# The values' round trip through DRAM: one copy in token order against eight copies by place and chunk, with the next values' load moved behind the reads

## The chip, the core and the metric

The kernel runs on one core of a Trainium2 chip. The metric is device time in microseconds; the kernel before takes 360.43 us (median of three runs, 359.46 to 362.16). One further execution was taken with the hardware profiler: 358.42 us, of which 356.7 us lie between its first and last instruction. All times inside the kernel are from that execution.

## What is computed

Chunked attention with a few memory keys, followed by a mixture of experts that gives every token its two best experts of eight. Cut to what matters:

```python
# attention: batch 4, heads 8, seq 768, head_dim 64, 8 memory keys
for c in range(24):                        # chunks of 32 queries
    l_start, r_end = max(0, 32*c - 16), min(768, 32*c + 32 + 8)
    k_full = concat(mem_k, k[l_start:r_end]); v_full = concat(mem_v, v[l_start:r_end])
    a = softmax(q[32*c:32*c+32] @ k_full.T / 8)
    out[32*c:32*c+32] = a @ v_full
# experts: 3072 tokens of 512, hidden size 1024
x = out.transpose(0, 2, 1, 3).reshape(3072, 512)
noisy = x @ w_gate + log1p(exp(x @ w_noise)) * noise
top2, weights = two largest of noisy, softmax over them
result = sum over the two experts e: weight * (relu(x @ w1[e]) @ w2[e])
```

Each chunk sees a window of 56 tokens: 16 to its left, its own 32, 8 to its right. With the 8 memory keys that makes 64 keys a chunk.

## The kernel before

The kernel has an attention stage and an expert stage. The attention stage runs over four batches of 768 tokens, each in three tiles of 256 tokens (twelve tiles, index `i`, in the loop at L562). For each tile TensorE makes the scores (`scores`, L402), VectorE takes the maximum and the difference (L423, L425), ScalarE the exponential (L430), TensorE turns the probabilities (`turn_p`, L433) and multiplies them by the values (`values`, L442, the product at L453), VectorE divides into the token rows (L460), and TensorE turns these and makes the gate's logits (`turn_x`, `gate`). The routing's small VectorE operations are strewn between the tiles. Then tokens are sorted by their pair of experts, gathered (L671), and sent through the two matmuls of the expert stage (L714, L726) and scattered to the output (L677).

Queries, keys and values of a batch are loaded by GpSimd's DMA queue with a conversion from float32 to bfloat16 (`load_nat`, L116; `load_v`, L119; `load_kq`, L122). A partition holds six neighbouring tokens of each head, so a piece in memory is 6 x 64 elements, 768 B once converted. Queries and keys are turned by TensorE (`turn`, L387, the transposes at L393) into `qT` and `kT`.

The values need no turning, but for the product at L453 the window of each chunk has to lie on the partitions: partition = place in the window, free axis = chunk and channel. The kernel makes this by a round trip through DRAM, in three steps:

- `spread_v` (L366, copies at L368): GpSimd brings the loaded values `vn` from head order into token rows of 512 channels, `vp`, in two copies, one for even and one for odd heads.
- `window_v`, first line (L374): one DMA on SP's queue writes `vp` to the DRAM tile `vd` (two of them, used in turn), as 16 rows of zeros, 768 token rows of 1 KB, 16 rows of zeros. A partition's six rows are one run of 6 KB. The zeros are written once at the start (L156).
- `window_v`, the rest: two DMAs put the memory values on 8 partitions (L378), and four DMAs read the windows back (L383, called spans below): for the even and the odd heads, the first 32 places and the last 24 places. One descriptor is 512 B, half a row; successive chunks of one place lie 32 rows (32 KB) apart. They fill `vb` (two of them, used in turn).

The order of transfers is set by the program order on the queues: `pin` keeps GpSimd's instructions as written, and SP's engine follows its written order too. GpSimd's order is: values, keys, queries of batch 0; spread 0; memory values and spans 0; values, queries, keys of batch 1; spread 1; **values of batch 2** (L535); then, at the first tile of batch b (L567 to L573): memory values and spans of b + 1; queries and keys of b + 2; spread of b + 2; **values of b + 3**. After the last spans come the loads of experts 0 to 2 (`load_expert`, L575, L578), later the gathers of tokens and the other experts, all on the same queue. The spans wait for SP's copy to have landed; SP's copy waits for the spread; the spread waits for the values.

`vn`, `vb` and the buffers of queries and keys lie in the part of the weights' tile `w_all` that later experts fill, which is why the profile shows loads, spans and products on `w_all`.

Of the kernel before, what the change touches and what calls it, by code (L numbers as in the profile page):

```python
# [12 lines left out]
BF16 = mybir.dt.bfloat16  # L13
# [9 lines left out]
def kernel(  # L23
# [14 lines left out]
    nc = tc.nc  # L38
    B, H, S, D = q.shape
# [30 lines left out]
    def pin(i):  # L70
        tc.keep_in_program_order(i)
# [36 lines left out]
    vn = scratch(H * SO * D).rearrange("p (h c) -> p h c", h=H)  # L108
    vb = [scratch(2 * NCH * HP * D).rearrange("p (a c w) -> p a c w", a=2, c=NCH) for _ in range(2)][::-1]
# [3 lines left out]

    vd = [tc.dram_tile([S + CH, Dm], BF16, name=f"vd{i}") for i in range(2)]

    def load_nat(t, x, b):  # L116
        pin(nc.gpsimd.dma_start(out=t, in_=x[b].rearrange("h (p s) d -> p h (s d)", s=SO)))

    def load_v(b):  # L119
        load_nat(vn, v, b)  # L120

    def load_kq(b):  # L122
        for x in ((1, 0) if b else (0, 1)):
            load_nat(nat[b % 2][x], (k, q)[x], b)
# [24 lines left out]
    nc.vector.tensor_copy(identf, identb[0:NG, 0:NG])  # L149
    vp = keep.tile([128, H * SO * D], BF16, name="vp")  # L150
    lg_all = keep.tile([128, NG, 2 * E], F32, name="lg_all")
    zeros = keep.tile([128, Dm], BF16, name="zeros")
    nc.vector.memset(zeros, 0.0)
    for i in range(2):
        for r0, n in ((0, LC), (LC + S, CH - LC)):
            nc.sync.dma_start(out=vd[i][r0:r0 + n, :], in_=zeros[0:n, :])  # L156


    mks = keep.tile([128, 2, D], F32, name="mks")
# [206 lines left out]
    def spread_v(b):  # L366
        for par in range(2):
            pin(nc.gpsimd.tensor_copy(  # L368
                out=vp.rearrange("p (s a c d) -> p a c s d", s=SO, a=2, c=HP)[:, par],
                in_=vn.rearrange("p (c a) (s d) -> p a c s d", a=2, s=SO)[:, par]))  # L370

    def window_v(b):
        t, o = vb[b % 2], vd[b % 2]
        nc.sync.dma_start(out=o[LC:LC + S, :].rearrange("(p s) c -> p (s c)", s=SO), in_=vp)  # L374
        for par in range(2):
            p0 = par * 64
            cols = slice(par * 256, (par + 1) * 256)
            pin(nc.gpsimd.dma_start(out=t[p0:p0 + NM, par], in_=mvn[b * NM:(b + 1) * NM, cols].unsqueeze(1).to_broadcast([NM, NCH, 256])))  # L378
        for par in range(2):
            p0 = par * 64  # L380
            cols = slice(par * 256, (par + 1) * 256)
            for r0, n in ((0, CH), (CH, WIN - CH)):
                pin(nc.gpsimd.dma_start(out=t[p0 + NM + r0:p0 + NM + r0 + n, par],  # L383
                                        in_=o[r0:r0 + S, cols].rearrange("(c k) w -> k c w", k=CH)[0:n]))

# [130 lines left out]
    with tc.manual_schedule(engines={ET.PE, ET.Activation, ET.DVE, ET.SP}):  # L516
# [17 lines left out]
        spread_v(1)  # L534
        load_v(2)  # L535
        pbs[0] = exps(scores(0))
# [25 lines left out]
        for i in range(NT):  # L562
# [423 lines left out]
```

## Time and profile before

| | |
|---|---|
| median of 3 runs | 360.43 us |
| profiled execution | 358.42 us |
| its span | 356.7 us |
| busy in the span: TensorE | 285.9 us (80%) |
| VectorE | 170.3 us (48%) |
| ScalarE | 136.9 us (38%) |
| GpSimd | 134.3 us (38%) |
| GpSimd's DMA queue (q0) | 34240 packets, 46.82 MB |
| SP's DMA queue (q1) | 13920 packets, 6.62 MB |
| mean granted clock of TensorE | 0.867 |

How to read it: the page gives busy time by engine, then the span in 40 slices of 8.9 us with a digit for the busy tenths of each. The attention stage fills the first 16 slices or so. A row of the timeline has start, duration, engine, line, operation, written and read tiles, and in brackets how long the engine had been idle and what ended that. A row of the DMA view for a window counts the packets that were moved in it; "software_dynamic" is GpSimd's queue, "hardware_dynamic" those of SP and ScalarE.

### The profile page before, as it was taken

What the parts mean: (1) busy time and instruction counts of PE and PEld (TensorE: products, weight loads), DVE (VectorE), ACT (ScalarE), POOL (GpSimd) and SP (SyncE); (2) the same over time, 40 slices, a digit from 0 to 9 for tenths busy, and PEclk for the clock granted to TensorE, in tenths of its full rate; (3) what the DMA queues carried; (4) which work ended last, traced back from release to release, by engine and by line L of the source; (5) the groups of instructions that cost most, each with busy time, mean ns of one, the idle gap of its engine ahead of it and who ended that gap; (6) DMA issues with size and microseconds to landing.
All of it is one profiled execution on the core that took longest, in us unless ns stands there. A gap on an engine that the chain in (4) does not pass through costs nothing.

```text
span 356.7 us, 7042 instructions
## 1 busy us (share of the span) xinstructions
PE 285.9 (80%) x2934; PEld 186.3 (52%) x2955; DVE 170.3 (48%) x349; ACT 136.9 (38%) x189; POOL 134.3 (38%) x181
## 2 busy tenths in 40 slices
PE   0356577777847732999999999999999999999991
PEld 0245455666736621865544465664455775565540
DVE  7656456699689885531133302954310334223221
ACT  8813645564645610144322343213243222243310
POOL 6460573354453036706530744332580122201122
PEclk9995655565687865699999999999999999999998
DMA  8999999999999999499999999961289971100012
GB/s 122 235 171 169 245 174 208 251 198 211 247 156 208 253 249 180 106 194 143 178 196 235 209 173 252 159 119 51 87 166 189 208 184 54 53 2 2 25 47 81
DMA packets 49866, 56.97 MB, mean 160 GB/s; under 512 B 16931, under 2 KB 39523, under 8 KB 49828
## 3 DMA queue, kind: packets, MB, share of 16 engines
q0 software_dynamic: 34240, 46.82, 73.2%
q1 hardware_dynamic: 13920, 6.62, 10.9%
q10 hardware_dynamic: 1668, 3.02, 2.4%
q8 instruction: 25, 0.41, 0.5%
q14 instruction: 13, 0.11, 0.1%
HBM read 70.39 MB, written 13.96 MB: 236 GB/s over the span
## 4 chain that ended last, share of the span: by engine, by line
PE 33%; issue 20%; POOL 5%; DVE 4%; DMA 3%; POOLq 1%; ACT 0%; DVEq 0%
PE p_h L714 18%; PE p_y L726 13%; POOL out_dram L677 4%; DMA out_dram<-y,main_dst 1%; DMA xTt<-xt 1%; DMA xt<-xd,main_src 1%; POOL xt L671 1%; DVE w_all L460 1%; PE p_xt L691 0%; POOL w_all L844 0%; POOLq L981 0%; DVE mx L423 0%; DVE sc L425 0%; ACT xT L472 0%; PE ps_o L453 0%
## 5 line engine op out<-in xcount | busy, mean ns | idle before, releaser
L714 PE MATMUL p_h<-xTt,w_all 128*128 128x256 bf16 (+3 forms) x669 | 102.7, 313 | 0.7 <-DVE xTt L692 0.5
L726 PE MATMUL p_y<-w_all,h 128*128 128x512 bf16 x446 | 102.3, 379 | 0.9
L714 PEld LDWEIGHTS <-w_all 128*128 128x128 bf16 x736 | 70.0, 101 | 36.3 <-issue 0.7
L702 ACT ACTIVATE h<-p_h 128x512 bf16<-128x512 f32 (+1 forms) x81 | 44.7, 551 | 95.9 <-PE p_h L714 88.3
L726 PEld LDWEIGHTS <-h 128*128 128x128 bf16 x464 | 45.3, 98 | 51.6
L700 DVE TENSOR_SCALAR h<-p_h 128x512 bf16<-128x512 f32 (+1 forms) x49 | 31.0, 633 | 82.8 <-PE p_h L714 73.7
L677 POOL DMA_INDIRECT out_dram<-y,main_dst x28 | 30.9, 1103 | 87.9 <-DVE y L732 75.4
L732 DVE SCALAR_TENSOR_TENSOR y<-p_y,main_w,y 128x512 f32<-128x512 f32 x28 | 21.0, 750 | 39.2 <-PE p_y L726 32.5
L393 PE MATMUL p_t<-identb,w_all 128*64 128x128 bf16 x384 | 20.6, 288 | 23.0 <-DMA w_all<-in_k_dram 13.4
L671 POOL DMA_INDIRECT xt<-xd,main_src x28 | 27.9, 997 | 24.2 <-DMA xTt<-xt 13.0
L730 ACT ACTIVATE y<-p_y,main_w 128x512 f32<-128x512 f32 x28 | 19.2, 687 | 37.0 <-PE p_y L726 36.0
L393 PEld LDWEIGHTS <-w_all 128*64 128x64 bf16 x384 | 18.1, 155 | 25.2 <-DMA w_all<-in_k_dram 13.9
L439 ACT COPY pT<-p_p 128x1024 bf16<-128x1024 bf16 x12 | 12.1, 1012 | 27.5 <-PE p_p L436 27.5
L383 POOL DMA_DIRECT2D w_all<-vd x16 | 11.8, 747 | 23.8 <-DMA vd<-vp 19.3
L460 DVE TENSOR_TENSOR w_all<-ps_o,rs 128x512 bf16<-128x512 f32 x24 | 15.6, 686 | 8.2 <-PE ps_o L453 7.8
L415 PE MATMUL ps_s<-kT,qT 128*32 128x112 bf16 x384 | 11.6, 276 | 7.2 <-DVE kT L549 5.4
L368 POOL COPY vp<-w_all 128x1536 bf16<-128x1536 bf16 x8 | 11.5, 1469 | 13.2 <-DMA w_all<-in_v_dram 13.2
L430 ACT ACTIVATE pb<-sc 128x1024 bf16<-128x1024 f32 x12 | 12.8, 1063 | 8.9 <-DVE sc L425 8.7
L549 DVE COPY kT<-p_t 64x768 bf16<-64x768 bf16 x12 | 11.5, 955 | 7.9 <-PE p_t L393 7.8
L425 DVE TENSOR_TENSOR sc<-ps_s,mx 128x1024 f32<-128x1024 f32 x12 | 14.7, 1225 | 0.8
L423 DVE TENSOR_REDUCE mx<-ps_s 128x16 f32<-128x1024 f32 x12 | 14.7, 1224 | 0.8 <-PE ps_s L415 0.5
L453 PE MATMUL ps_o<-w_all,pT 128*32 128x128 bf16 x384 | 10.9, 280 | 3.3 <-issue 2.0
(172 smaller groups left out, 284.0 us busy)
## 6 DMA issues: line engine op xcount, KB each, us to landing
w_all<-in_moe_w_dram POOLq DMA_DIRECT2D x16, 1024.0 KB, 20.7
w_all<-in_moe_w_dram POOLq DMA_DIRECT2D x8, 512.0 KB, 13.8
w_all<-in_v_dram POOLq DMA_DIRECT2D x4, 768.0 KB, 12.1
w_all<-in_k_dram POOLq DMA_DIRECT2D x4, 768.0 KB, 20.9
w_all<-in_q_dram POOLq DMA_DIRECT2D x4, 768.0 KB, 18.1
vd<-vp SPq DMA_DIRECT2D x4, 768.0 KB, 9.0
w_all<-vd POOLq DMA_DIRECT2D x8, 384.0 KB, 13.0
w_all<-vd POOLq DMA_DIRECT2D x8, 288.0 KB, 13.3
```

What stands on the lines that cost most here:

```text
L393: nc.tensor.transpose(out=p_t[own(par), s, :], in_=src[:, 2 * pair + par, s * D:(s + 1) * D], identity=identb, tile_position=(0, par * 64))
L423: nc.vector.tensor_reduce(out=mx, in_=s3, axis=AX, op=Alu.max)
L425: nc.vector.tensor_tensor(out=sc, in0=s3, in1=bc(mx, KW), op=Alu.subtract)
L460: nc.vector.tensor_tensor(out=xr[:, j, 0:Dm].rearrange("p (h d) -> p h d", h=H), in0=ps_o[:, j].rearrange("p c a d -> p (c a) d"), in1=bc( ...
L671: i = nc.gpsimd.indirect_dma_start(out=xts[key].bitcast(I32), out_offset=None, in_=xd, in_offset=bass.IndirectOffsetOnAxis(ap=ix, axis=0))
L677: i = nc.gpsimd.indirect_dma_start(out=out, out_offset=bass.IndirectOffsetOnAxis(ap=ix, axis=0), in_=y, in_offset=None, bounds_check=N - 1 ...
L700: nc.vector.tensor_scalar(out=out_, in0=in_, scalar1=0.0, scalar2=None, op0=Alu.max)
L702: nc.scalar.activation(out=out_, in_=in_, func=Act.Relu)
L714: nc.tensor.matmul(out=o, lhsT=w(kp * F + f * 128, 128), rhs=x[:, kp], start=(kp == 0), stop=(kp == KP - 1))
L726: nc.tensor.matmul(out=p, lhsT=h[:, (f * n + j) * 128:(f * n + j + 1) * 128], rhs=w(KP * F + f * Dm, Dm), start=(f == 0), stop=(f == FB - 1))
L730: nc.scalar.activation(out=y, in_=p, func=Act.Copy, scale=weight)
L732: nc.vector.scalar_tensor_tensor(out=y, in0=p, scalar=weight, in1=y, op0=Alu.mult, op1=Alu.add)
```

## The change

Three things are changed together.

1. The values are loaded with eight neighbouring tokens to a partition, on 96 partitions instead of 128 (`SV`, `VP`). A piece is 1 KB once converted. The spread copies 2048 elements on 96 partitions instead of 1536 on 128.
2. `vd` is ordered by place in the chunk, then chunk: eight groups of four places, each group with 4 x 24 rows of 1 KB and 2 rows of padding. The write to it becomes eight DMAs on SP, each of 24 partitions with four rows of 1 KB. A span's successive chunks are then successive rows, 1 KB apart; a span still has descriptors of 512 B, its source has the eight (or six) groups as its outermost dimension, and the order of the four spans is changed (first 32 places of both halves, then the last 24 of both). The places of the left neighbour's tokens are written one row further, so that the last 24 places are read by the same rule from one row further. The zeros fill the first row of the first four groups and the last of the others; they are written after the loads of the memory values.
3. The values of batch b + 2 are loaded at the first tile of batch b, between the spans of b + 1 and the queries and keys of b + 2. Before, they were loaded one step earlier, ahead of those spans.

```diff
+    SV = 8
+    VP = S // SV
+    vn = scratch(H * SV * D).rearrange("p (h c) -> p h c", h=H)
...
-    vd = [tc.dram_tile([S + CH, Dm], BF16, name=f"vd{i}") for i in range(2)]
+    VG = 4 * NCH + 2
+    vd = [tc.dram_tile([CH // 4, VG, Dm], BF16, name=f"vd{i}") for i in range(2)]
...
     def load_v(b):
-        load_nat(vn, v, b)
+        pin(nc.gpsimd.dma_start(out=vn[0:VP], in_=v[b].rearrange("h (p s) d -> p h (s d)", s=SV)))
...
-    for i in range(2):
-        for r0, n in ((0, LC), (LC + S, CH - LC)):
-            nc.sync.dma_start(out=vd[i][r0:r0 + n, :], in_=zeros[0:n, :])
...
         nc.sync.dma_start(out=mvs[b * NM:(b + 1) * NM], in_=mem_v[b].rearrange("h m d -> m h d"))
+    for i in range(2):
+        for g0, x in ((0, 0), (LC // 4, VG - 2)):
+            nc.sync.dma_start(out=vd[i][g0:g0 + LC // 4, x], in_=zeros[0:LC // 4, :])
...
             pin(nc.gpsimd.tensor_copy(
-                out=vp.rearrange("p (s a c d) -> p a c s d", s=SO, a=2, c=HP)[:, par],
-                in_=vn.rearrange("p (c a) (s d) -> p a c s d", a=2, s=SO)[:, par]))
+                out=vp.rearrange("p (s a c d) -> p a c s d", s=SV, a=2, c=HP)[0:VP, par],
+                in_=vn.rearrange("p (c a) (s d) -> p a c s d", a=2, s=SV)[0:VP, par]))
...
     def window_v(b):
         t, o = vb[b % 2], vd[b % 2]
-        nc.sync.dma_start(out=o[LC:LC + S, :].rearrange("(p s) c -> p (s c)", s=SO), in_=vp)
+        for x in range(CH // SV):
+            c0, g = divmod(LC // SV + x, CH // SV)
+            for z in range(2):
+                nc.sync.dma_start(out=o[2 * g + z, c0:c0 + 4 * NCH].rearrange("(k c) w -> c k w", c=NCH),
+                                  in_=vp[x:VP:CH // SV, z * 4 * Dm:(z + 1) * 4 * Dm].rearrange("p (k w) -> p k w", w=Dm))
...
-        for par in range(2):
-            p0 = par * 64
-            cols = slice(par * 256, (par + 1) * 256)
-            for r0, n in ((0, CH), (CH, WIN - CH)):
-                pin(nc.gpsimd.dma_start(out=t[p0 + NM + r0:p0 + NM + r0 + n, par],
-                                        in_=o[r0:r0 + S, cols].rearrange("(c k) w -> k c w", k=CH)[0:n]))
+        for x, n in ((0, CH), (1, WIN - CH)):
+            for par in range(2):
+                p0 = par * 64 + NM + x * CH
+                cols = slice(par * 256, (par + 1) * 256)
+                pin(nc.gpsimd.dma_start(out=t[p0:p0 + n, par].rearrange("k c w -> k (c w)"),
+                                        in_=o[0:n // 4, x:x + 4 * NCH, cols]))
...
         load_kq(1)
         spread_v(1)
-        load_v(2)
...
                 window_v(b + 1)
                 if b + 2 < B:
+                    load_v(b + 2)
                     load_kq(b + 2)
                     spread_v(b + 2)
-                if b + 3 < B:
-                    load_v(b + 3)
```

More of the change, by code (lines that the diff above doesn't have):

```diff
@@ L107 @@
     xrow = [scratch(SO * Dm).rearrange("p (s r) -> p s r", s=SO) for _ in range(2)]
-    vn = scratch(H * SO * D).rearrange("p (h c) -> p h c", h=H)
+    SV = 8
+    VP = S // SV
+    vn = scratch(H * SV * D).rearrange("p (h c) -> p h c", h=H)
     vb = [scratch(2 * NCH * HP * D).rearrange("p (a c w) -> p a c w", a=2, c=NCH) for _ in range(2)][::-1]
@@ L149 @@
     nc.vector.tensor_copy(identf, identb[0:NG, 0:NG])
-    vp = keep.tile([128, H * SO * D], BF16, name="vp")
+    vp = keep.tile([128, SV * Dm], BF16, name="vp")
     lg_all = keep.tile([128, NG, 2 * E], F32, name="lg_all")
```

## The prediction

> **What bounds the kernel now.** I read the page first, then a table of windows, then the timelines of TensorE, GpSimd and the other engines, and at the end the DMA view cut into windows in which one kind of transfer runs alone.
>
> ```profile
> PE 285.9 (80%) x2934; PEld 186.3 (52%) x2955; DVE 170.3 (48%) x349; ACT 136.9 (38%) x189; POOL 134.3 (38%) x181
> DMA  8999999999999999499999999961289971100012
> ```
> ```profile
> 40.00:50.00 10.00, 6.01 (x116) 5.18 (x111) 2.80 (x3) 6.08 (x8) 5.22 (x8) 0.51 1.20 229
> 80.00:90.00 10.00, 7.69 (x165) 6.21 (x164) 9.27 (x17) 5.15 (x6) 4.58 (x10) 0.50 1.23 212
> 130.00:140.00 10.00, 2.63 (x25) 1.85 (x25) 8.27 (x35) 0.00 (x0) 4.75 (x9) 0.50 1.10 207
> 150.00:175.00 25.00, 24.84 (x153) 14.49 (x154) 6.07 (x11) 10.09 (x18) 9.27 (x10) 1.00 1.07 174
> ```
>
> The window columns are length, busy time of PE, PEld, DVE, ACT and POOL, granted clock, DMA share, GB/s. From 150 us the expert stage is TensorE alone (24.84 of 25 us), and the change touches nothing there. Before it, the DMA engines are full all the time (share over 1), while the computing engines are not until about 80 us; then VectorE is (9.27 of 10). So the attention stage is bound by transfers first and by VectorE later, and what the change can move is when the expert stage starts. TensorE's timeline shows where transfers are waited for:
>
> ```profile
> 13.89 2.13 PE L393 MATMUL p_t<-identb,w_all 128*64 128x128 bf16 x36 [8.54 <-DMA w_all<-in_k_dram]
> 20.33 2.77 PE L393 MATMUL p_t<-identb,w_all 128*64 128x128 bf16 x48 [3.03 <-DMA w_all<-in_q_dram]
> 32.79 1.04 PE L453 MATMUL ps_o<-w_all,pT 128*32 128x128 bf16 x32 [1.30 <-DMA w_all<-vd]
> 39.77 2.43 PE L393 MATMUL p_t<-identb,w_all 128*64 128x128 bf16 x48 [1.25 <-DMA w_all<-in_q_dram]
> 45.62 2.13 PE L393 MATMUL p_t<-identb,w_all 128*64 128x128 bf16 x36 [3.43 <-DMA w_all<-in_k_dram]
> 61.15 1.04 PE L453 MATMUL ps_o<-w_all,pT 128*32 128x128 bf16 x32 [2.03 <-issue]
> 68.03 1.49 PE L393 MATMUL p_t<-identb,w_all 128*64 128x128 bf16 x24 [2.63 <-DMA w_all<-in_q_dram]
> 71.05 3.40 PE L393 MATMUL p_t<-identb,w_all 128*64 128x128 bf16 x60
> 98.57 1.46 PE L393 MATMUL p_t<-identb,w_all 128*64 128x128 bf16 x36 [1.44 <-DMA w_all<-in_k_dram]
> 143.04 0.59 PE L691 MATMUL p_xt<-identb,xt 128*128 128x128 bf16 x4 [3.74 <-DMA xt<-xd,main_src]
> ```
>
> Keys come at 45.62 and 98.57, two batches apart: 26.5 us a batch. The waits of batches 1 and 2 (1.30, 1.25, 3.43, 2.03, 2.63) are real; that at 98.57 is covered, since VectorE's key copies begin only at 101.77, with no wait:
>
> ```profile
> 101.77 3.87 DVE L549 COPY kT<-p_t 64x768 bf16<-64x768 bf16 x4
> ```
>
> GpSimd's timeline gives the order in which the transfers are queued:
>
> ```profile
> 9.62 2.87 POOL L368 COPY vp<-w_all 128x1536 bf16<-128x1536 bf16 x2 [2.83 <-DMA w_all<-in_v_dram]
> 19.97 2.96 POOL L383 DMA_DIRECT2D w_all<-vd  x4 [4.95 <-DMA vd<-vp]
> 35.95 2.88 POOL L368 COPY vp<-w_all 128x1536 bf16<-128x1536 bf16 x2 [10.34 <-DMA w_all<-in_v_dram]
> 39.14 0.88 POOL L117 DMA_DIRECT2D w_all<-in_v_dram  x1 [0.30 <-POOL vp L368]
> 45.77 2.96 POOL L383 DMA_DIRECT2D w_all<-vd  x4 [4.42 <-issue]
> 66.19 2.96 POOL L383 DMA_DIRECT2D w_all<-vd  x4 [8.95 <-DMA vd<-vp]
> 137.47 1.61 POOL L671 DMA_INDIRECT xt<-xd,main_src  x1 [2.24 <-DVE facts L307]
> ```
>
> **Spans.** Per batch two of 384 KB and two of 288 KB are read back, 1.376 MB. The DMA view of five windows, in this order: spans alone in batches 1 and 2, half a microsecond in batch 0's first span, loads alone, the copy to vd beside a load.
>
> ```profile
> DMA packets 216, 0.65 MB, mean 162 GB/s; under 512 B 58, under 2 KB 58, under 8 KB 216
> ```
> ```profile
> DMA packets 245, 0.75 MB, mean 187 GB/s; under 512 B 63, under 2 KB 63, under 8 KB 245
> ```
> ```profile
> DMA packets 37, 0.15 MB, mean 295 GB/s; under 512 B 1, under 2 KB 1, under 8 KB 37
> ```
> ```profile
> DMA packets 811, 0.61 MB, mean 204 GB/s; under 512 B 13, under 2 KB 811, under 8 KB 811
> ```
> ```profile
> q1 hardware_dynamic: 110, 0.68, 84.7%
> q0 software_dynamic: 124, 0.09, 29.9%
> ```
>
> The spans run at 162 to 187 GB/s, so 1.376 MB take 7.4 to 8.5 us (8.0). The copy moved 0.68 MB in its 2 us, 340 GB/s. The pieces of a span are 512 B before and after; what changes is that one engine's successive pieces lie 1 KB apart instead of 32 KB. Ends for the new time: 8.0 us, if the piece is what costs, and 4.05 us at the copy's rate. That 512-B pieces can go faster is seen in the 295 GB/s window; I take 330 GB/s, 4.2 us, a saving of 3.8 a batch. The Trainium skill, DMA: Bandwidth & Descriptors, section Latency and other measured facts, speaks against it: its copies keep 207 GB/s at a row pitch of 512 KiB and fall to 103 only at 4 MiB, by which 32 KB would not be the brake and the spans would stay at 8.0. No run here separates the two.
>
> **Spread.** Two copies of 1.44 us a batch grow from 1536 to 2048 elements a partition: 2 x 1.96 = 3.9, so 1.0 later, all of it between the values' landing and the copy to vd.
>
> **Copy to vd.** One issue becomes eight on SP.
>
> ```profile
> L374 SPq DMA_DIRECT2D vd<-vp x4: 319/334/355, 12.5 to 80.2; - x4
> DMA to landing us min/median/max: 7.2/9.0/10.9
> ```
>
> Seven more issues are 7 x 0.33 = 2.3 us, on a queue that has nothing else to do then. The copy and a load alternated packet by packet above (110 and 124 in 2 us). With 1-KB packets a load in flight costs the copy more turns, and the copy costs the load fewer bytes. Ends for issue to landing: 7.2 (all hidden) and 10.9 + 2.3 + 0.6 = 13.8, the 0.6 if an issue takes 0.42, as some zero fills do:
>
> ```profile
> L156 SPq DMA_DIRECT2D vd<-zeros x4: 332/420/1475, 1.9 to 3.2; - x4
> ```
>
> I take 7.2 + 2.3 = 9.5, and 8.0 in batch 0, where the last load is nearly through and the issues overlap the delay that the copy has anyway. GpSimd's spans wait for all eight, and the next loads are queued behind them.
>
> **Loads of values.** 768 rows of 1 KB replace 1024 of 768 B; at the load's bytes per microsecond (0.61 MB in 3 us) each takes 3.9 us either way: nothing. Values of batches 2 and 3 move from ahead of the spans to behind them, same bytes: the spans come 3.9 us sooner in the queue, but the queue runs empty while the copy lands, where it worked before. Three more numbers are needed, from the DMA view: the slices of 0.175 us from 19 to 26 us, a small load, the write of xd.
>
> ```profile
> DMA  9997990000000389966689999896959979498959
> ```
> ```profile
> mks<-in_mem_k_dram SPq DMA_DIRECT2D x1, 64.0 KB, 2.1
> xd<-w_all ACTq DMA_DIRECT2D x3, 768.0 KB, 7.8
> ```
>
> From the spans' issue at 19.97 to data (the zeros) pass 1.3 to 1.5 us: 1.5. Even 64 KB land only after 2.1 us; half of that, 1.0, I estimate for the landing after a load's last byte. The xd write is as large as the copy: 2.3 us at 340 GB/s, less 0.3 for the load bytes that pass beside it, 2.0. Now every batch is a chain: values 3.9 + landing 1.0, spread 4.0, copy 9.5, first data 1.5, spans 4.2 = 24.1 us, against 26.5 before. The zero fills' move at the start hides behind the first loads (8.54 us of waiting for keys).
>
> **The sum.** Batch 0: spans issued at 19.97 + 1.0 + 0.8 = 21.8, over 3.8 sooner: values, queries of batch 1 come 2.0 earlier (queries at 37.8, before 39.77). Keys took 5.85 us behind them for a 3.9-us load, as the copy took 2; with 1-KB turns about 1: 3.0 earlier, 42.6. Batch 1: values 33.95, spread 37.9, copy landed 47.4, spans 48.9 to 53.1, ready before TensorE asks (61.15 - 2.03 - 3.0 = 56.1). Queries of batch 2: 53.1 + 3.9 + 3.9 + 2.0 (the xd write that falls there) + 1.0 = 63.9, before 68.03; keys 63.9 + 3.9 + 1.0 = 68.8, before used from about 72.0 in the row at 71.05: 3.2 earlier. Batch 2: spans end at 53.1 + 24.1 = 77.2, keys of batch 3 at 77.2 + 11.7 + 4.0 = 92.9, needed at 98.57 - 1.44 - 3.2 = 93.9: no wait. From here VectorE keeps the 3.2. Spans of batch 3 end at 101.3. Before they were issued from 90.44 and took 14.9 us to land, until about 106:
>
> ```profile
> 90.44 2.96 POOL L383 DMA_DIRECT2D w_all<-vd  x4 [5.43 <-DMA vd<-vp]
> ```
> ```profile
> w_all<-vd POOLq DMA_DIRECT2D x2, 288.0 KB, 14.9
> ```
>
> So they and the expert loads behind them come some 4 us sooner; the first gather, behind those loads, waits 0.5 less of its 3.74. Sum 3.7 us. Against the profiled execution (358.42 us, span 356.7; 2.0 below the median 360.43) that is 354.7; against the median, 356.7.
>
> **Rivals.** B, the spans do not speed up: 512-B pieces cost 43 ns wherever they lie. For it: every batch shows 162 to 187 GB/s. Against it: at the start 1156 packets, nearly all under 512 B, went in 1 us on 16 engines, 14 ns each.
>
> ```profile
> DMA packets 1156, 0.11 MB, mean 113 GB/s; under 512 B 1150, under 2 KB 1156, under 8 KB 1156
> ```
>
> Then batch 0 is 1.8 late and a batch's chain is 27.9: spans of batch 1 end at 60.7, queries 71.5, keys 76.4 (4.4 late), spans of batch 3 end at 116.5, 10.5 us late, the expert loads with them, and the gathers wait behind these: 4.4 to 10.5 slower, 365 to 371. It decides where spans take over 6 us.
>
> D, spans on half the engines, ends the same way. At half of 340 GB/s the 1.376 MB take 8.1 us, and the price is B's. The Trainium skill, same page, section Why a DMA increments its semaphore by 16 and not by 1, gives each copy the largest number up to 16 that divides both outermost sizes: eight and six engines for the spans, twelve for the copy to vd. By its round-robin cursor the two halves fall on different engines and the rate holds; no row here shows engines.
>
> C, the copy to vd lands after 13.8 us, with fast spans: a chain of 28.4, spans of batch 1 end at 57.4, keys of batch 2 at 73.1, 1.1 late, those of batch 3 about 1 late, spans of batch 3 at 114.2: 1 to 8 slower, 361 to 368. From about 11.5 the gain is gone. Opposite: if it lands in 7.2 and spans take 4.05, the queries of batch 2 cease to be waited for and keys come over 5 us earlier: 354.
>
> **How the numbers follow.** The forecast's case has 0.55, with a range of its own of 353 to 360; 1% (3.6 us, about what a measurement can tell) cuts it into 0.44 faster and 0.11 within. C has 0.18 (0.08 within, 0.10 slower), B and D 0.27, all slower. Faster 0.44, same 0.19, slower 0.37. The time is that of the likeliest case, 356.7. The range is 353 to 367: from the best ends into B's lower half, leaving out some 0.2.
>
> **What would show it.** Spans alone in a DMA window at over 290 GB/s (right) or under 200 (B, D); SP's copies landing within 9.5 us of the first issue, or later (C); keys on TensorE near 42.6, 68.8 and 93; a queue with idle stretches ahead of each batch's spans; first transposes of the expert stage near 139.3. If the stage after that differs from before by more than 1 us, something else moved and the argument is wrong.

## The result, and the profile after

The changed kernel takes 387.83 us (median of 4 runs, 384.94 to 389.6), the kernel before 360.81 us on the same chip (4 runs, 359.46 to 362.16): a ratio of 1.074, 95% interval 1.066 to 1.082. The forecast was 356.7 us, with a range to 367. The profiled execution took 389.6 us with a span of 388.0 us. Medians below are of all runs of a kernel, while ratios leave out the runs that fell into a slower state of the chip, so a ratio need not be that of the two medians.

The page, busy shares and the DMA row of the slices:

```profile
PE 281.3 (72%) x2934; PEld 182.1 (47%) x2955; DVE 170.9 (44%) x349; ACT 136.9 (35%) x189; POOL 141.1 (36%) x181
DMA  8939938993899599995989999997129993100002
```

TensorE does the same work, but its share has fallen from 80% to 72%. The row of the DMA engines now has three 3s and a 5 among its first 18 slices, where it had only 8s and 9s in the first 16: the transfers stop between batches. TensorE's timeline, with the wait and its releaser in brackets:

```profile
37.53 1.05 PE L458 MATMUL ps_o<-w_all,pT 128*32 128x128 bf16 x32 [9.33 <-DMA w_all<-vd]
44.59 2.77 PE L398 MATMUL p_t<-identb,w_all 128*64 128x128 bf16 x48 [1.33 <-DMA w_all<-in_q_dram]
75.55 1.04 PE L458 MATMUL ps_o<-w_all,pT 128*32 128x128 bf16 x32 [14.84 <-DMA w_all<-vd]
83.62 1.49 PE L398 MATMUL p_t<-identb,w_all 128*64 128x128 bf16 x24 [3.82 <-DMA w_all<-in_q_dram]
109.36 1.05 PE L458 MATMUL ps_o<-w_all,pT 128*32 128x128 bf16 x32 [8.56 <-issue]
119.85 1.00 PE L353 MATMUL p_list<-vals,oh_l 128*128 128x168 bf16 x6 [9.13 <-POOL vals L343]
175.31 0.58 PE L694 MATMUL p_xt<-identb,xt 128*128 128x128 bf16 x4 [4.88 <-DMA xt<-xd,main_src]
```

The first product with the values (ps_o) of batch 0 stands at 37.53 (32.79 before), of batch 1 at 75.55 (61.15), of batch 2 at 109.36 (88.55); the list product follows at 119.85 (89.76, with no wait). The expert stage begins 32.3 us later, 175.31 against 143.04, and takes as long as before (388.0 - 175.31 = 212.7; 356.7 - 143.04 = 213.7). All of the loss is ahead of it, in waits for the values' window and one wait for GpSimd. (For the 8.56 us at 109.36 the profile names no releaser; that batch's spans were issued at 95.84 to 99.78, as GpSimd's rows below show.) SP's timeline, cut at each batch, and GpSimd's show where these come from:

```profile
13.53 9.29 SPq L378 DMA_DIRECT2D vd<-vp  x8
44.61 9.22 SPq L378 DMA_DIRECT2D vd<-vp  x8
82.47 9.42 SPq L378 DMA_DIRECT2D vd<-vp  x8
116.34 9.49 SPq L378 DMA_DIRECT2D vd<-vp  x8
```
```profile
25.14 3.94 POOL L388 DMA_DIRECT2D w_all<-vd  x4 [9.71 <-DMA vd<-vp]
57.77 3.95 POOL L388 DMA_DIRECT2D w_all<-vd  x4 [11.92 <-DMA vd<-vp]
95.84 3.94 POOL L388 DMA_DIRECT2D w_all<-vd  x4 [12.12 <-issue]
112.59 3.73 POOL L369 COPY vp<-w_all 96x2048 bf16<-96x2048 bf16 x2 [10.21 <-DMA w_all<-in_v_dram]
117.92 1.88 POOL L343 TENSOR_TENSOR vals<-ohp,facts 128x1008 bf16<-128x1008 bf16 x1
128.49 3.94 POOL L388 DMA_DIRECT2D w_all<-vd  x4 [7.38 <-DMA vd<-vp]
```

Eight issues hold SP for 9.2 to 9.5 us, and the spans are issued 11.6, 13.2, 13.4 and 12.2 us after the first of them. From one batch's spans to the next pass 32.6, 38.1 and 32.7 us, where the forecast had 24.1. In the first of these 15.7 us lie between the spans' issue (25.14) and the next spread (40.85), where the forecast had 10.6 (first data 1.5, spans 4.2, values 3.9, landing 1.0), 3.7 are the spread (4.0 in the forecast), and 13.2 go from the first copy's issue to the next spans (9.5 in the forecast). The DMA view of two windows: spans alone in batch 0 (27 to 31 us), and the end of batch 1's copies.

```profile
DMA packets 407, 0.75 MB, mean 187 GB/s; under 512 B 226, under 2 KB 226, under 8 KB 407
```
```profile
DMA packets 15, 0.01 MB, mean 3 GB/s; under 512 B 5, under 2 KB 15, under 8 KB 15
```

The spans run at 187 GB/s, as before. In the second window, 55 to 59 us, the queue is empty: values of the next batch are queued behind spans that GpSimd hasn't issued yet.

### The profile page after: what moved, and what is told of

The parts are those of the page before. It is cut to its first block, busy times and chain, and to the rows that moved or that the text cites. A ratio compares the mean times of both kernels' runs of the same rounds, so it can differ in the third digit from the quotient of the medians.

```text
span 388.0 us, 7086 instructions
## 1 busy us (share of the span) xinstructions
PE 281.3 (72%) x2934; PEld 182.1 (47%) x2955; DVE 170.9 (44%) x349; ACT 136.9 (35%) x189; POOL 141.1 (36%) x181
## 4 chain that ended last, share of the span: by engine, by line
PE 31%; issue 18%; POOL 5%; DMA 3%; DVE 3%; ACT 1%; POOLq 1%; ACTq 0%
PE p_h L717 16%; PE p_y L729 12%; POOL out_dram L680 3%; DMA out_dram<-y,main_dst 1%; POOL xt L674 1%; DMA xTt<-xt 1%; DMA xt<-xd,main_src 1%; DVE w_all L465 1%; ACT pT L444 0%; PE ps_o L458 0%; PE p_xt L694 0%; POOL w_all L847 0%; PE p_list L353 0%; POOLq L984 0%; ACT xT L477 0%
## 5 line engine op out<-in xcount | busy, mean ns | idle before, releaser
L680 POOL DMA_INDIRECT out_dram<-y,main_dst x28 | 30.9, 1102 | 91.0 <-DVE y L735 72.5
L458 PE MATMUL ps_o<-w_all,pT 128*32 128x128 bf16 x384 | 11.1, 285 | 32.7 <-DMA w_all<-vd 24.2
L398 PE MATMUL p_t<-identb,w_all 128*64 128x128 bf16 x384 | 18.5, 263 | 20.4 <-DMA w_all<-in_k_dram 8.1
L388 POOL DMA_DIRECT2D w_all<-vd x16 | 15.8, 993 | 41.1 <-DMA vd<-vp 29.0
L369 POOL COPY vp<-w_all 96x2048 bf16<-96x2048 bf16 x8 | 14.9, 1888 | 36.8 <-DMA w_all<-in_v_dram 36.8
L398 PEld LDWEIGHTS <-w_all 128*64 128x64 bf16 x384 | 15.7, 138 | 22.8 <-DMA w_all<-in_k_dram 9.5
L458 PEld LDWEIGHTS <-pT 128*32 128x32 bf16 x384 | 8.5, 128 | 33.0 <-issue 32.8
L420 PE MATMUL ps_s<-kT,qT 128*32 128x112 bf16 x384 | 10.9, 269 | 6.0 <-DVE kT L553 4.8
```

The lines of the kernel that those rows point to most:

```text
L388: pin(nc.gpsimd.dma_start(out=t[p0:p0 + n, par].rearrange("k c w -> k (c w)"), in_=o[0:n // 4, x:x + 4 * NCH, cols]))
L398: nc.tensor.transpose(out=p_t[own(par), s, :], in_=src[:, 2 * pair + par, s * D:(s + 1) * D], identity=identb, tile_position=(0, par * 64))
L458: nc.tensor.matmul(out=ps_o[r * CH:(r + 1) * CH, j, pair], lhsT=pT[:, j * HP + pair, r * CH:(r + 1) * CH], rhs=vb[b % 2][:, :, (tp * 2 + j ...
L680: i = nc.gpsimd.indirect_dma_start(out=out, out_offset=bass.IndirectOffsetOnAxis(ap=ix, axis=0), in_=y, in_offset=None, bounds_check=N - 1 ...
```

## The experiments

After this profile the theory was: the copies are the loss (an issue costs 0.75 us and not 0.33, and a late copy now delays the next values as well), with the order of loads behind it. Rivals: the spans' new form, with eight groups outermost; the memory values' transfers, which run while SP issues; and GpSimd's routing operations, queued behind a spread that waits for later values.

Two measures are used. The ratio is of whole times, against the kernel before on the same chip. The start of the expert stage (first p_xt on TensorE) is read from one profiled execution, and uncertain by several microseconds: the kernel with the routing first, below, equals the changed kernel up to the first product of batch 1, and has it at 69.73 where the changed kernel has 75.55. (Its spans follow each other by 31.0, 33.1 and 32.1 us, so that the 38.1 above belongs to that one execution.) The runs are also from several chips, on which the kernel before took 360.2 to 364.3 us.

| kernel | ratio (95% interval) | expert stage from, us |
|---|---|---|
| before | 1 | 143.04 |
| 96 partitions, one copy, old spans, old order | 1.010 (1.005 to 1.015) | 147.46 |
| one copy, changed spans, old order | not usable | 147.10 |
| eight copies, changed spans, old order | 1.035 (1.032 to 1.039) | 160.40 |
| four stepped copies, pitch of 33 rows, old order | 1.025 (1.016 to 1.035) | 156.02 |
| before with the changed order | 1.012 (1.001 to 1.023) | 150.38 |
| the same, routing first | 1.006 (1.002 to 1.010) | 150.46 |
| one copy, changed spans, changed order | not usable | 157.45 |
| four stepped copies, spans from 32 rows, changed order | 1.041 (1.037 to 1.046) | 159.71 |
| changed kernel | 1.074 (1.066 to 1.082) | 175.31 |
| changed, routing first | 1.063 (1.053 to 1.072) | 169.19 |
| changed, neighbouring partitions | 1.055 (1.048 to 1.063) | 164.17 |
| changed, both of these | 1.054 (1.045 to 1.063) | 166.24 |

**Copy and spans without the order.** The changed kernel with load_v where it was before.

```
+        load_v(2)
...
-                    load_v(b + 2)
...
+                if b + 3 < B:
+                    load_v(b + 3)
```

> The changed copy and spans, with the values' loads put back where the kernel before had them (ahead of the spans). Theory 1 (eight copies to vd hold SP 0.75 us each and land 11 to 13 us after the first issue, and the new order makes each us of that a us of the batch): values are then in place early, the chain is cut, 362 to 370 us. Rival 2 (the order alone did it, the copy is harmless): 357 to 362 us. Rival 3 (the spans on eight engines did it): 378 us or more, since the spans are the same.

377.21 us against 364.25 on that chip, 1.035: outside all three expected ranges, between the first theory's and the third's. So about half of the loss comes without the order. What the theories left out is that here loads run beside the copies. In batch 2 SP issues its eight in 6.35 us, with no issue held, and the spans still come 15.7 us after the first of them:

```profile
67.92 6.35 SPq L378 DMA_DIRECT2D vd<-vp  x8
83.60 3.94 POOL L388 DMA_DIRECT2D w_all<-vd  x4 [13.29 <-DMA vd<-vp]
```

The DMA view from 72 to 80 us shows the copies' 1-KB packets taking turns with the loads; below it, from 64 to 69 us, is one copy of 8-KB rows beside loads, in batch 2 of the run with one copy and the old order further down, where the spans come 9.6 us after the issue:

```profile
q0 software_dynamic: 1475, 1.14, 91.5%
q1 hardware_dynamic: 755, 0.69, 32.8%
```
```profile
q0 software_dynamic: 478, 0.38, 46.8%
q1 hardware_dynamic: 112, 0.79, 39.1%
```

The eight copies move 0.69 MB in 8 us, the one copy 0.79 MB in less than 5.

**The order alone.** The kernel before with the opposite of that edit.

> The kernel before, with only the values' loads moved behind the spans. Theory 1: the copy lands in 7 to 10 us as before, a batch is values 4.9, spread 3, copy 9, first data 1.5, spans 8, so 26.4 us, about the 26.5 of before: 360 to 367 us. Rival 2: most of the 27 us, 378 us or more. Rival 3: 360 us, as the spans are those of before.

368.76 us, 1.012: the first theory's 360 to 367, on a chip on which the kernel before takes 364.25. The products of batches 1 and 2 come no later than before, but the list product now waits. TensorE's timeline:

```profile
99.08 1.00 PE L352 MATMUL p_list<-vals,oh_l 128*128 128x168 bf16 x6 [9.20 <-POOL vals L342]
```

The two edits add up to 4.7% when each is measured alone (3.3 to 6.1 by the ends of the intervals), and cost 7.4% together (6.6 to 8.2).

**Spans from 32 rows, and the old places at another pitch.** The first keeps the changed kernel's order and stores a row for each of 32 places, so that the spans have 32 outermost rows; the second keeps token order and the old order of loads, with 33 rows of 1 KB from chunk to chunk. Both copy with four transfers of 24 stepped partitions. The first edit is cut from the difference to the changed kernel, the second from that to the kernel before:

```
-    vd = [tc.dram_tile([CH // 4, VG, Dm], BF16, name=f"vd{i}") for i in range(2)]
+    VG = NCH + 2
+    vd = [tc.dram_tile([CH, VG, Dm], BF16, name=f"vd{i}") for i in range(2)]
```
```
-    vd = [tc.dram_tile([S + CH, Dm], BF16, name=f"vd{i}") for i in range(2)]
+    VG = CH + 1
+    vd = [tc.dram_tile([NCH + 1, VG, Dm], BF16, name=f"vd{i}") for i in range(2)]
```

> The changed kernel with vd by place (26 rows each) instead of by groups of four: the spans' source has 32 or 24 as its outermost size, as before the change, and successive chunks stay 1 KB apart; the copy is four DMAs of 24 x 8 rows of 1 KB. Rival 3: spans at 290 GB/s or more, a saving of some 4 us a batch, 372 to 378 us. Theory 1 with a price per DMA: SP is held half as long (3 us a batch), 376 to 381 us; with a price per row: four issues of about 1.5 us, no change in the copy, 384 to 389 us unless the spans gain.

> Token order as before, but with 33 rows from chunk to chunk instead of 32, so that a span's successive pieces lie 33 KB apart; values on 96 partitions, the copy is four DMAs of 24 runs of 8 KB, values' loads ahead of the spans as before. If the 32-KB pitch is what holds the spans: 250 GB/s or more in windows with spans alone, 350 to 357 us. If the 512-B piece is: 160 to 190 GB/s as before, 359 to 364 us. Theory 1 with a price per row: an issue of 24 runs takes 0.35 us or less.

379.52 us (1.041) and 373.65 us (1.025). The DMA view while the spans run alone, of the first from 87 to 91 us, of the second from 57 to 61 us:

```profile
DMA packets 245, 0.76 MB, mean 191 GB/s; under 512 B 59, under 2 KB 59, under 8 KB 245
```
```profile
DMA packets 259, 0.82 MB, mean 204 GB/s; under 512 B 60, under 2 KB 60, under 8 KB 259
```

At a pitch of 32 KB, 33 KB and 1 KB, with eight groups or 32 rows outermost, the spans run at 162 to 204 GB/s: the pitch is not what costs. The second kernel missed the 359 to 364 us that were expected for that case, since its issues stayed dear: four cost as much apiece as eight, 0.75 us (median) in the first and 0.70 in the second. With four copies for eight and 32 rows for eight groups the ratio falls from 1.074 to 1.041, the largest gain of any edit to the changed kernel whose time can be read. The spans follow the first issue by 10.9, 10.3, 11.1 and 7.4 us; how much of the gain is the copies' and how much the spans' is not separated.

**Transfers by themselves.** A program that computes nothing of the reference issues single transfers of these shapes, three of each.

> Not the kernel: it computes nothing of the reference, and writes zeros and loaded values as its output. Each transfer three times by itself, the next after the last has landed. Reads of 768 pieces of 512 B from DRAM on GpSimd's queue: into 32 partitions with pieces 32 KB apart (L37), 1 KB apart on sixteen engines (L39) and from eight groups (L41), then the same pieces into 64 (L43) and 128 partitions (L45); 384 pieces of 1 KB into 32 (L47) and 128 partitions (L50). If the pitch is the brake: L37 some 2 us longer than L39. If the piece is: L37, L39, L43, L45 alike, L47 and L50 shorter. If the number of partitions written is (a limit on the SBUF side): L37, L39, L41 and L47 alike, L45 and L50 shorter by 1 us or more. L55: the first form on GpSimd's and SP's queue at once, into two different sets of 32 partitions: twice the rate if the limit is on the SBUF side. SP's copies to DRAM: 128 partitions (as before) issue in 0.33 us; 24 partitions with rows of 1 KB (as changed) and with one run of 8 KB, spaced by four or side by side, 32, 96 and 16 partitions: theory 1 with a price per DMA that hangs on the 24 partitions says 0.70 to 0.75 for 24 in all forms, and about 0.33 for 16, 32 and 96. L53 against L75: a memory-value copy alone, and beside a 128-partition copy: if the two hold each other, both land 2 us or more later together.

Its answers for three span reads on GpSimd's queue (old pitch; 1 KB with 32 outer rows; eight groups as in the changed kernel):

```profile
L37 POOL DMA_DIRECT2D t<-in_v_dram x3: 715/731/870, 7.6 to 16.6; - x3
DMA to landing us min/median/max: 4.1/4.1/4.3
```
```profile
L39 POOL DMA_DIRECT2D t<-in_v_dram x3: 715/715/715, 20.9 to 30.4; - x3
DMA to landing us min/median/max: 4.4/4.4/4.5
```
```profile
L41 POOL DMA_DIRECT2D t<-in_v_dram x3: 982/993/1008, 35.1 to 46.4; - x3
DMA to landing us min/median/max: 5.3/5.4/5.4
```

The old pitch lands first. The groups' form costs 0.28 us more to issue and 1.0 us more to land than the same rows in 32 places. What else holds the spans stays open: the same bytes landed after 3.7 us on 128 partitions and 3.8 us in 1-KB pieces, against 4.1, so neither the number of partitions nor the piece explains the rate by itself. A memory-value copy landed after 4.4 us alone and 5.2 beside one copy of 128 partitions: 0.8 us later, where 2 or more were named as the sign of the two holding each other, and SP's single issue was not held there (0.32 us). The reads meant to run on two queues at once hardly overlapped; the run with two queues below stands for them. And SP's issue durations (ns, minimum, median, maximum) for 24 partitions in steps of four, with 1-KB pieces and then whole 8-KB rows; 24 neighbours; 32 in steps of four:

```profile
L60 SPq DMA_DIRECT2D dd<-src x3: 745/756/937, 126.1 to 130.9; - x3
```
```profile
L62 SPq DMA_DIRECT2D dd<-src x3: 704/718/762, 133.3 to 139.1; - x3
```
```profile
L64 SPq DMA_DIRECT2D dd<-src x3: 290/306/338, 142.0 to 147.0; - x3
```
```profile
L68 SPq DMA_DIRECT2D dd<-src x3: 448/464/509, 157.1 to 161.7; - x3
```

The dear issue needs the step between partitions, since 24 neighbours take 0.31 us, and does not hang on the pieces. With the step the count matters too: 24 partitions cost more than 32 (0.72 against 0.46 us), for which no run here has a reason.

**Memory values behind the spans.** The changed kernel with line 383's two transfers issued after line 388's four.

> The changed kernel with the two memory-value copies of a batch put behind its spans, so that they do not run beside SP's eight copies. Theory 1, in its present form (SP held 0.75 us by each copy, and 2.5 to 3 us more while memory values are on the engines): SP issues in 6.4 us instead of 9.4, spans 3 us sooner in each of four batches, 8 to 13 us faster than the changed kernel: 1.035 to 1.05 of before. If the memory values only happen to run then: no change, 1.07 of before.

389.18 us, 1.084 (1.075 to 1.093): the expected gain failed. SP's eight issues did shorten to 6.3 to 6.7 us, the spans followed the first of them by 8.9 to 9.3 us (11.6 to 13.4 in the changed kernel) and went out 3 to 6 us sooner (22.27, 54.62, 90.25, 123.90), but TensorE then waited for the memory values:

```profile
70.79 1.04 PE L458 MATMUL ps_o<-w_all,pT 128*32 128x128 bf16 x32 [8.52 <-DMA w_all<-mvn]
```

So it shows that the memory values hold SP's issues and delay the copies by 2.7 to 4.3 us a batch, but not what that costs the kernel.

**Two queues.** The kernel before with the spans of the odd half on SP's queue.

> The kernel before, with the odd heads' spans issued from SP instead of GpSimd. If spans are held on the SBUF side (32 or 24 partitions written at a time), both halves now run at once into different partitions: spans of a batch in 4.5 to 6 us instead of 8, 3 to 8 us faster than before. If the 512-B pieces are the cost, or DRAM: no change in the spans, within 2 us of before.

The ratio is 0.997 (0.990 to 1.005). The DMA view from 21 to 25 us, both queues at spans:

```profile
q0 software_dynamic: 166, 0.42, 55.2%
q1 hardware_dynamic: 811, 0.41, 47.9%
```

They share 210 GB/s, little above the 191 and 204 GB/s of one queue, and the time does not change. SP's moves its 0.41 MB in packets of 512 B.

**96 partitions.** The kernel before with eight tokens on each of 96 partitions and one copy of 96 rows.

```
-        nc.sync.dma_start(out=o[LC:LC + S, :].rearrange("(p s) c -> p (s c)", s=SO), in_=vp)
+        nc.sync.dma_start(out=o[LC:LC + S, :].rearrange("(p s) c -> p (s c)", s=SV), in_=vp[0:VP])
```

> The kernel before, with values on 96 partitions of eight tokens instead of 128 of six, one copy of 96 runs of 8 KB to vd in token order. Theory 1: the spread is 0.9 us longer, the copy one issue: 1 to 4 us slower than before, so that the 96 partitions do not explain the loss. If they do: 8 us or more.

361.95 us, 1.010, within the 1 to 4 us expected: the 96 partitions do not explain the loss.

**Routing first, in both kernels.** The spread of batch 3 goes behind the routing operations of tiles 0 to 5 on GpSimd.

```
-                    spread_v(b + 2)
+                    if b == 0:
+                        spread_v(2)
...
                 r0.values(nc.gpsimd, 0, NV)
+                spread_v(3)
```

> The changed kernel with GpSimd's routing operations of tiles 0 to 5 (line 300 to line 343) ahead of the spread of batch 3 instead of behind it; nothing else moves. In the changed kernel the list product waits 9.13 us for them at 119.85. Theory 1 (one chain of values, spread, copy and spans sets the end; the routing wait lies beside it): the list product's wait goes to under 1 us, but batch 3's spans still land at about 137 to 138 us and its product, at 139.06 without a wait before, now waits 6 to 8 us for them; the time falls by 1 to 3 us only, to a ratio of 1.065 to 1.072. Theory 2 (the routing wait is a loss of its own beside the late spans): the time falls by 8 to 9 us, a ratio of 1.045 to 1.055, with no new wait at the product.

> The kernel before with the changed kernel's order of loads alone (1.012 in the first comparison), and now the routing operations ahead of batch 3's spread. Theory 1: the list product's 9.20-us wait at 99.08 goes; batch 3's spans landed at about 112 and its product began at 117.91 without a wait, so some 6 us of the 9.2 can be kept: ratio 0.992 to 1.000, and the whole cost of the order was this wait. Theory 2 (the order costs by itself, since values leave HBM later and their queue runs empty): the ratio stays at 1.008 to 1.012 with the wait moved to batch 3's product.

The changed kernel falls to 385.82 us, 1.063. TensorE's timeline:

```profile
104.05 1.00 PE L353 MATMUL p_list<-vals,oh_l 128*128 128x168 bf16 x6
135.26 1.04 PE L458 MATMUL ps_o<-w_all,pT 128*32 128x128 bf16 x32 [5.40 <-DMA w_all<-vd]
```

The list product's wait is gone, and 5.40 us of it come back at batch 3's product: the first theory's wait, with a gain between the two. In the kernel before with the changed order (366.01 us, 1.006) the list product moves from 99.08 to 90.71 without a wait, yet the expert stage begins where it did (150.46 and 150.38): batch 3's queries, which this order loads behind the spans, are waited for 3.15 us at 97.35, and the first gather 5.76 us. The forecast of 0.992 to 1.000 failed; the ratio lies between the theories.

**Neighbouring partitions.** The changed kernel's copies read 24 neighbours, so that the values land in the wrong places.

```
-                                  in_=vp[x:VP:CH // SV, z * 4 * Dm:(z + 1) * 4 * Dm].rearrange("p (k w) -> p k w", w=Dm))
+                                  in_=vp[x * NCH:(x + 1) * NCH, z * 4 * Dm:(z + 1) * 4 * Dm].rearrange("p (k w) -> p k w", w=Dm))
```

> The changed kernel with its eight copies reading 24 neighbouring partitions each in place of every fourth; same number of transfers, rows and bytes, but the values land in the wrong places, so the values' part of the output is not the reference's. Theory 1 (the issue price of 0.75 us hangs on the stepped partitions, and a late copy delays each following batch's values): an issue takes 0.29 to 0.36 us and SP's eight 4.5 to 6 us with the memory values' stall in them (9.2 to 9.5 before); the spans start 3 to 4 us sooner in batch 0 and 9 to 12 us sooner in batch 3; the ratio falls from 1.074 to 1.035 to 1.05. Theory 2 (the copy is bound by its 3072 packets of 1 KB, about 5.2 us at the 150 GB/s seen): the issues end sooner but the copy lands only 1 to 2 us sooner; ratio 1.06 to 1.07. Theory 3 (the price hangs on the pieces of 1 KB): issue stays at 0.75 us and nothing changes.

> Both edits: neighbouring partitions in the copies (values land in the wrong places, so their part of the output is not the reference's) and the routing operations ahead of batch 3's spread. Theory 1 (one chain): 1 to 4 us below the kernel with the neighbours alone, a ratio of 1.025 to 1.045, and batch 3's product waits for its spans again. Theory 2 (losses add): 9 us below it, a ratio of 1.01 to 1.025.

382.84 us, 1.055. The issues by their duration, and SP's timeline in batches 0 and 3:

```profile
L378 SPq DMA_DIRECT2D vd<-vp x32: 290/394/4944, 13.5 to 111.7; - x32
```
```profile
13.51 8.54 SPq L378 DMA_DIRECT2D vd<-vp  x8
107.90 4.19 SPq L378 DMA_DIRECT2D vd<-vp  x8
```

The median issue falls from 0.753 to 0.394 us, but in batches 0 to 2 one issue is held for 4.0 to 4.9 us (2.5 to 3.2 in the changed kernel) while the memory values run. Only in batch 3, where the memory values are issued as SP finishes, are the eight done in 4.2 us. The price of an issue was right, the gain fell between the first theory (1.035 to 1.05) and the second (1.06 to 1.07): the spans followed the first issue by 11.2, 11.2, 10.4 and 10.0 us, in batch 3 only 2.2 us sooner than in the changed kernel though SP was done 5.3 us sooner. So the price of the issues is not all that makes the copies late. With the routing first as well, 382.74 us, 1.054: no further gain, so the losses do not add. The range of 1.025 to 1.045 was missed because it stood on the gain of the neighbours, which fell short.

**Without the memory values, and with one copy.** Line 383's transfers left out for batches 2 and 3, in the changed kernel and in the kernel before; and one copy in place of the eight, in both orders.

```
-        for par in range(2):
+        for par in range(2 if b < 2 else 0):
```
```
-        for x in range(CH // SV):
...
+        nc.sync.dma_start(out=o.rearrange("g v w -> (g v w)")[0:S * Dm].rearrange("(p x) -> p x", p=VP), in_=vp[0:VP])
```

> The changed kernel with the memory values' two transfers (line 383) left out for batches 2 and 3, so that these batches multiply the memory values of batches 0 and 1: that part of the computation is not done. Theory 1 (the memory values' 48 packets hold SP's copies for 2.5 to 3.2 us, and that is on the chain): SP's eight issues take 6.0 to 6.4 us in batches 2 and 3 in place of 9.2 to 9.5, the spans start 3 us sooner in batch 2 and 6 us sooner in batch 3, and the ratio falls to 1.055 to 1.062. Theory 2 (the hold lies beside the copies' own packets): the issues are shorter but the spans start where they did, ratio 1.068 to 1.08.

> The kernel before with the same transfers left out for batches 2 and 3 (that part of the computation is not done). Theory 1: its one copy is issued in 0.33 us and loses little to the memory values, and its products of batches 2 and 3 wait for nothing (88.55 and 108.72 without a wait): ratio 0.993 to 1.000. Theory 2 (the collision costs every version alike): 0.983 to 0.99, as large as the gain of the changed kernel from the same edit.

> The changed kernel with one copy of 96 rows of 8 KB per batch, written as one piece of DRAM, in place of the eight; the spans read as in the changed kernel, so the values land in the wrong places and their part of the output is not the reference's. Theory 1 (the eight copies and what follows from them are the loss): the copy lands 6 to 9 us after its issue (11.6 to 13.3 in the changed kernel), ratio 1.015 to 1.035, which is the order (1.012) and the 96 partitions (1.010) and some 0.25 us for each span's issue. Theory 2 (the spans on eight engines cost as much as the copies): ratio 1.045 to 1.06.

> The same one copy and the changed kernel's spans, with the order of loads of the kernel before; the values land in the wrong places. The kernel with 96 partitions, one copy and the old spans stood at 1.010. Theory 1: the form of the spans costs only its dearer issue, 4 times 0.25 us, and lands neither sooner nor later: ratio 1.008 to 1.02. Theory 2 (eight engines carry the spans slower): 1.025 to 1.04. Theory 3 (the spans gain, as predicted for the change, 3.8 us a batch): 0.985 to 1.0.

All four took 1175 to 1196 us, and none of the expected ratios can be read. The changed values send other tokens to the experts, and the loop for tokens beyond a pair's block runs some 20 times; the costliest groups of the kernel before without memory values show it:

```profile
L831 DVE TENSOR_TENSOR scr<-kt,io_l 128x3072 bf16<-128x3072 f32 x23 | 77.2, 3359 | 53.9 <-DMA out_dram<-scr,t_dst 53.9
```

The attention stage runs ahead of that loop and issues the same instructions whatever the values, so its traces can be read up to the expert stage. Without memory values in the changed kernel, SP in batches 2 and 3, and the spans on GpSimd:

```profile
77.76 6.86 SPq L378 DMA_DIRECT2D vd<-vp  x8
109.59 6.35 SPq L378 DMA_DIRECT2D vd<-vp  x8
```
```profile
87.16 4.02 POOL L388 DMA_DIRECT2D w_all<-vd  x4 [9.43 <-PE p_t L398]
118.41 4.05 POOL L388 DMA_DIRECT2D w_all<-vd  x4 [5.34 <-PE p_t L398]
```

From the first issue to the spans 9.4 and 8.8 us pass, against 13.4 and 12.2: 4.0 and 3.4 us are the memory values' hold, at least, since the spans' last wait is now put down to TensorE and no longer to the copies. The expert stage begins at 166.30, 9.0 us sooner, of which up to 5.8 may be the difference between two executions noted above. In the kernel before the same edit gives 2.0 us (141.03). With one copy, changed order:

```profile
62.21 1.04 PE L453 MATMUL ps_o<-w_all,pT 128*32 128x128 bf16 x32 [4.41 <-DMA w_all<-vd]
92.58 1.05 PE L453 MATMUL ps_o<-w_all,pT 128*32 128x128 bf16 x32 [4.21 <-issue]
104.90 1.00 PE L352 MATMUL p_list<-vals,oh_l 128*128 128x168 bf16 x6 [10.96 <-POOL vals L342]
157.45 0.58 PE L689 MATMUL p_xt<-identb,xt 128*128 128x128 bf16 x4 [1.63 <-DMA xt<-xd,main_src]
```

The spans follow the issue of the copy by 9.1, 6.6, 7.9 and 6.4 us, and the expert stage begins 17.9 us sooner than with eight. In the old order the difference is 13.3 us (160.40 to 147.10), and 147.10 is where the old spans stand too (147.46): the new form gains nothing that this measure could show. Nor does it show a cost, in the old order; in the changed order 7.1 us lie between one copy with the old spans (150.38) and with the new (157.45), of which the 96 partitions explain 4.4 by the old order's rows.

No version here was faster than the kernel before by more than its interval.

## Why the prediction was wrong

- **Spans, 8.0 to 4.2 us: failed.** The step "what changes is that one engine's successive pieces lie 1 KB apart instead of 32 KB" made the pitch the brake. The spans ran at 187 GB/s in place of the 330 taken, and no pitch tried made them faster. The 3.8 us a batch that carried the forecast do not exist. Rival B had the unchanged rate, though its reason, the piece of 512 B, is not shown; and the sentence on the Trainium skill (DMA: Bandwidth & Descriptors, Latency and other measured facts) was the one to believe: at 32 KB and 33 KB no penalty is seen here either. Of the two rows set against B, the 295 GB/s window held half a microsecond, and the 1156 packets in 1 us had some 95 B each (0.11 MB).
- **Spans on half the engines (rival D): the issue was dearer, 0.99 us, in the kernel the price did not show.** By itself one such read lands 1.0 us later; in the old order the start of the expert stage does not tell the forms apart (147.10 and 147.46). That fits the Trainium skill's rule as the prediction told it (same page, Why a DMA increments its semaphore by 16 and not by 1), by which the two halves fall on different engines; no row here shows engines.
- **Copy, 7 x 0.33 = 2.3 us: failed.** The price came from a copy of 128 neighbouring partitions. Twenty-four in steps of four cost 0.75 us, and while the memory values run one issue stands for 2.5 to 3.2 us: 9.2 to 9.5 us on SP, 6.3 to 6.7 without them. The forecast said that SP "has nothing else to do then", and did not look at what shares the DMA engines with it. Issue to spans was 11.6 to 13.4 us where 8.0 and 9.5 were taken: rival C's case. That it came near C's 13.8 is luck: C had a load in flight and issues of 0.42 us, and in the changed kernel it was the stepped partitions and the memory values. The copies' own term, that 1-KB packets beside a load cost the copy more turns, was given next to no price; where such a load runs (copy and spans without the order) the spans came 15.7 us after the first issue.
- **Sum and rivals: B and C came true together,** and each had been priced with the other's forecast in place. The chain of 24.1 us plus 3.8 for the spans and some 3 for the copy is 30.9 a batch; 32.6 to 38.1 were seen, and 31.0 to 33.1 with the routing first. They were taken one at a time, and so was the range. The forecast was right that the order makes one chain of each batch and that the queue runs empty; it fits this that order and copies cost 7.4% together and 1.2% and 3.5% apart. In the old order the next values are queued ahead of the spans and load while the copy is on its way; that a late copy then costs only its own batch is argued from the order of the queue.
- **Not in the prediction at all:** GpSimd's routing operations stand behind the spread of batch 3, and the spread waits for values that the change loads later. The list product waits 9.13 us. By the routing-first run this is worth about 1% (1.074 to 1.063, intervals that overlap), since batch 3's product waits in its place.
- **Spread, + 1.0: right for its step** (3.73 against 2.87 us); with 96 partitions and the 8-KB rows the ratio is 1.010.
- **Expert stage unchanged to 1 us: right** (212.7 and 213.7).

By starts of the expert stage the 32.3 us are: 96 partitions 4.4, the spans' form -0.4, the eight copies 13.3, the order on top of them 14.9 (in which up to 5.8 may be the one execution). By whole times the steps are 1.0% for the 96 partitions, 2.5% for form and copies together and 3.9% for the order on top of them, some 4, 9 and 14 us. Open remains how the copies' cost divides between issue, hold and the 1-KB packets: neighbouring partitions and no memory values were tried one by one, and not together.

## What to carry to other kernels

Before a transfer is split, look at which partitions each part reads and what else is on the DMA engines while it is issued: a price from a contiguous transfer does not hold for a stepped one. When a load is moved behind a step that waits, write out the whole chain from one batch to the next, and price the rivals together as well as singly, since each late step then lengthens every following batch. On an in-order queue, list what stands behind the waiting instruction, even if it belongs to another stage.

## What the runs showed of the hardware

- Issuing a copy from SBUF on SP's queue took 0.30 to 0.34 us (medians) for 16, 24, 32, 96 or 128 neighbouring partitions, 0.46 for 32 in steps of four and 0.70 to 0.75 for 24 in steps of four, whether it had 24 rows of 8 KB, 96 of 1 KB or 192.
- A broadcast of memory values inside SBUF, two transfers with 48 packets of 4 KB in all, took 1.1 to 1.3 us a packet (median of each batch) in the changed kernel and 0.7 us by itself. Where its packets moved while SP was issuing four or eight copies, one issue stood for 2.3 to 5.1 us.
- Reads of 512-B pieces ran at 162 to 210 GB/s, over windows of 4 us, in every layout, order and number of queues tried.
- A copy from SBUF to DRAM in 768 packets of 1 KB moved 0.69 MB in 8 us beside loads, one in 96 packets of 8 KB 0.79 MB in less than 5 us.
